# Opening a three-part kernel another way, and placing a block's last output product inside the next block

## The chip, the cores and the metric

The kernel runs on 1 core of one Trainium2 chip. The metric is the device time of one execution in microseconds. Before the change three runs took 1523.68 to 1529.89 us, with a median of 1525.85 us. All arithmetic is in fp32; a matrix product is either done on whole fp32 operands (such a matmul stands as one in the program and as two in the trace) or as three products of operands cut into a high and a low part.

## The reference, cut to what matters

Three parts follow one another. The first is a two-way attention between a sequence `x` (8 batches, 8 heads, 512 positions, 64 columns) and a small state (32 rows per head); its output has 8 x (512 + 32) rows of 512 columns. The second is a gated MLP with 1536 hidden columns, the third an MLP with 2048.

```python
scores = scale * np.matmul(x, state.transpose(0, 1, 3, 2))
scores = scores - scores.max(-1, keepdims=True)
a = np.exp(scores)
a /= a.sum(-1, keepdims=True) + 1e-09
xread = np.matmul(a, state)
scores2 = scale * np.matmul(state, x.transpose(0, 1, 3, 2))
...
sread = np.matmul(a2, x)
return np.concatenate([xread, sread], axis=2).astype(np.float32)

g = x @ w_gate
silu = g * (1.0 / (1.0 + np.exp(-g)))
val = x @ w_val
return (silu * val @ w_out).astype(np.float32)

h = x @ w_in
g = h * (1.0 / (1.0 + np.exp(-1.702 * h)))
return (g @ w_out).astype(np.float32)
```

The weights of the two MLPs arrive as 64-bit floats and are turned into fp32 on the chip.

## The kernel before, in words

The work is split into nine blocks of rows: one for each batch's 512 positions (blocks 0 to 6, then 7 at the end) and, before the last, a block "B" with the 256 state rows of all batches. A block goes through 12 steps `f` of the first MLP. A step makes a gate product and a value product (`product`, the value one after the gate one, each into a `gv` bank of PSUM), takes Silu of the gate on ScalarE, multiplies on VectorE into `h`, cuts `h` into a high part (ScalarE) and a low part (VectorE, in block 0 GpSimd), and then issues the output product `out1` of the step before: four output tiles `acc0` to `acc3`, three matmuls of 128x512 each. The output product of step 11 closes the block; `evac` then copies the four tiles out and SyncE stores them. After the nine blocks the second MLP runs over the same blocks, from about 798 us to the end; the change does not touch it.

Attention for batch b+1 is prepared during block b. It is written in pieces: two groups of four heads, each with a load of `x` (`xn`), transpositions (`turn0`, `turn1`), scores (`scores0`, `scores1`, or `scores_full` for the first two batches), maxima along the state (`max_n`) and along the sequence (`max_s`), exponentials (`exp_n`, `exp_s`), sums, and the reads of the state. Three hand-written tables set the order: `START` lists what happens before block 0 (groups A0 and A1 of batch 0), `BLOCK0` places the pieces of batch 1, and of A0 and A1's remaining work, at places (f, 0), (f, 1), (f, 2) of block 0, and `GROUP` does so for all later batches. Place 0 comes after Silu, place 1 after the multiplication, place 2 after the output product. Every engine executes its own instructions strictly in the order in which they are written.

Three more things share these places. A `slot` (`whole_slot`) starts the 64-to-32-bit turn of one raw weight tile (two ScalarE activations, L200 and L201), finishes the one before (VectorE L209 and L210, GpSimd L213) and issues the load of another; block 0 has three slots in each step (`beside`), and before it START has its own. `state_weights` multiplies the turned gate and value weights (`wf`) with the state (`st`), since batch 0 multiplies attention weights with these products; each needs two turned tiles. A `quad_job` does the same for batches 1 to 7, with two PSUM tiles at a time; the lists `JOBS` say at which third of a step it stands, and a job at place 0 follows the pieces of `GROUP` at that place.

PSUM's eight banks are four `acc`, two `gv` and two `at`. Transpositions, scores, state products and quad jobs ask for an `at` tile through `at()`; a list `extra` lets `at()` hand out the `acc` banks too, until `extra.clear()` at the end of START.

SyncE and ScalarE issue the DMAs, each in its own order. Lines that the prediction speaks of: L426 transposes `xn`, L380 the raw state, L534 the exponentials of the state scores (`e`), whose copy to SBUF is `ec` at L537; L334 is any whole product; L624 a quad job; L446 and L447 the scores of a later batch; L327 to L329 gate and value products; L923 to L925 the output product; L948 is Silu, L961 the multiplication, L776 and L777 the cut of `h`; L487 and L488 are `max_s`, L502 is `exp_s`.

Of the kernel before, what the change touches and what calls it, by code (L numbers as in the profile page):

```python
# [8 lines left out]
F32 = mybir.dt.float32  # L9
# [8 lines left out]


START = """  # L20
A0.load0 A0.load1 states weights1 A1.load0 A1.load1 weights6 G0.load
A0.turn0 A0.turn_h0 A0.turn1 A0.turn_h1 attn_state slot slot A0.scores_full
A1.turn0 A1.turn_h0 A1.turn1 A1.turn_h1 slot A0.max_n A0.less_max:v A0.exp_n A1.scores_full slot
A1.max_n A1.less_max:v A1.exp_n slot sw0 A0.sum_n A0.over_sum:v A0.back_full sw1
A1.sum_n A1.over_sum:v A1.back_full slot slot A0.max_s A1.max_s A0.exp_s A1.exp_s slot
""".split()

BLOCK0 = {  # L30
    (0, 1): "A0.turn_e",
    (0, 2): "A1.turn_e",
    (1, 0): "G0.turn0 G0.turn_h0",
    (1, 1): "A0.state_read",
    (1, 2): "attn_state",
    (2, 0): "A0.state_sum A1.state_read G0.turn1 G0.turn_h1",
    (2, 2): "A1.state_sum G0.scores_full",
    (3, 0): "G0.max_n G0.max_s",
    (3, 2): "A0.state_store A1.state_store G0.less_max:v G0.exp_n G0.exp_s",
    (4, 0): "G0.sum_n G0.over_sum:v G0.turn_e",  # L40
# [14 lines left out]
}  # L55
GROUP = {
    (0, 1): "turn0 turn_h0 turn_l0:v",
    (1, 0): "scores0",
    (1, 1): "turn1 turn_h1 turn_l1:v",
    (1, 2): "scores1",  # L60
    (2, 0): "max_n",
    (2, 1): "less_max:v max_s",
# [10 lines left out]
def kernel(  # L73
# [29 lines left out]
    P = 128  # L103
    KD = DM // P
    F1 = FF1 // P
    U1 = F1 // 2
    F2 = FF2 // P
    J = S // P
# [5 lines left out]
    v, a, pe, pool_e, sy = nc.vector, nc.scalar, nc.tensor, nc.gpsimd, nc.sync  # L114
# [6 lines left out]
    dp = ctx.enter_context(tc.tile_pool(name="scratch", bufs=1, space=DRAM))  # L121
# [219 lines left out]
    def accs():  # L341
        return [psa.tile([P, 512], F32, name=f"acc{i}", tag=f"acc{i}") for i in range(4)]
# [25 lines left out]
    def load_states(qd, q=sy):  # L368
        sb["raw"] = sb_raw = ap.tile([P, HP, P], F32, name="sb_raw", tag="e2")
        for j in range(4):  # L370
            q.dma_start(
                sb_raw[j * NS : (j + 1) * NS].rearrange("n hp (hl d) -> n hp hl d", hl=2),
                state[4 * qd + j].rearrange("(hp hl) n d -> n hp hl d", hl=2),
            )
# [276 lines left out]
    def cut_fetched(b, u, g, home=None):  # L651
# [6 lines left out]

    JOBS = [
        [10, 14, 17, 20, 22, 24, 26, 29, 30, 31, 32, 33, 34, 35],  # L660
        [2, 6, 7, 8, 9, 10, 12, 13, 15, 17],
        range(0, 36, 3),
        range(0, 36, 3),
    ]
# [118 lines left out]
    def evac(acc, N):  # L783

        for e in range(0, len(acc), 2):
            ev = work.tile([P, 2, 512], F32, name="ev", tag="raw", bufs=RAWS)
            a.copy(ev[:, 0, :N], acc[e][:, :N])
            v.tensor_copy(ev[:, 1, :N], acc[e + 1][:, :N])
            yield e, ev

    def h_tile(n):
# [10 lines left out]
    groups[0, 0], groups[0, 1] = A0, A1  # L802
    groups[1, 0] = Group(1, 0, whole=True)
    named = {"A0": A0, "A1": A1, "G0": groups[1, 0]}
    more = {
        "attn_state": lambda: (turn_states(0), attn_state(0)),
        "slot": whole_slot,
        "sw0": lambda: state_weights(0, 0),
        "sw1": lambda: state_weights(0, 1),
        "states": lambda: load_states(0, a),  # L810
    }
    for n in range(1, 7):
        more[f"weights{n}"] = lambda n=n: w_dma(n)
    for word in START:
        piece(word, named, more)()
    extra.clear()

    tails = []

# [44 lines left out]
    def cut_units(u, ks=range(KD)):  # L864

        for k in ks:
# [2 lines left out]
            a.copy(w[:, 0, :], t)  # L869
            pool_e.tensor_tensor(w[:, 1, :], t, f32(w[:, 0, :]), op=ALU.subtract)  # L870

    order2 = [B] + list(range(B))
    for i, blk in enumerate(order1):
        tail = blk == B
# [20 lines left out]
        def run(f, place):  # L895
            move()
            for fn in plan.pop((f, place), []):
                fn()

        nxt = None  # L900
        if not last and order1[i + 1] == B:
            nxt = tail_x
        acc = [] if i == 0 else accs()
        hs = {}

        def out1(f, between=None, k0=0):
            if not acc:
                acc.extend(accs())
            if i == 0:
                need_whole(("o", 0, f))  # L910
                cut_outs()
            h = hs.pop(f)
            w = units["o", 0 if i == 0 and f == 1 else 1, f]
            pos["outs"] = f + 1
            for e in range(KD):
                c = slice(e * P, (e + 1) * P)
                ps = acc[e][:, :N]
                if i == 0 and f == 1:
                    pe.matmul(ps, w[:, c], f32(h[:, 0, :N]), start=f == 0, stop=f == F1 - 1)
                    if between and e % 2 == 1:  # L920
                        between(k0 + e // 2)
                    continue
                pe.matmul(ps, w[:, 0, c], h[:, 0, :N], start=f == 0, stop=False)  # L923
                pe.matmul(ps, w[:, 1, c], h[:, 0, :N], start=False, stop=False)  # L924
                pe.matmul(ps, w[:, 0, c], h[:, 1, :N], start=False, stop=f == F1 - 1)  # L925
                if between and e % 2 == 1:
                    between(k0 + e // 2)
# [14 lines left out]
        for f in range(F1):  # L942
# [3 lines left out]
            beside()  # L946
            sg = work.tile([P, 512], F32, name="sg", tag="sg")
            a.activation(sg[:, :N], pg[:, :N], ACTF.Silu)  # L948
            run(f, 0)
            if i == 0 and f % 2 == 1 and f < F1 - 2:  # L950
                state_weights(f // 2 + 1, 1)
# [30 lines left out]
                need(units2[min(NEW + 2 * f + 1, len(units2) - 1)][0])  # L982
                x2_step(0, f, 1)
        assert not plan
        out1(F1 - 1, nxt, 2)
        y1[blk] = []
        for e, ev in evac(acc, N):
            y = dp.tile([P, 2, N], F32, name=f"y1_{blk}_{e}")
            sy.dma_start(y, ev[:, :, :N])
            y1[blk].append(y)  # L990
        if i == 3:
            pos["limit"] = where["i2", 0]
            w_dma(2)
# [299 lines left out]
```

## Time and profile before

| | |
|---|---|
| median of 3 runs | 1525.85 us |
| profiled execution, its own time | 1525.99 us |
| span of its instructions | 1524.2 us |
| PE busy | 1484.9 us |
| DVE busy | 925.9 us |
| ACT busy | 686.1 us |
| POOL busy | 395.3 us |
| mean granted TensorE clock | 0.996 |

PE is TensorE's matmuls, PEld its weight loads, DVE VectorE, ACT ScalarE, POOL GpSimd, SP SyncE. The span runs from the first to the last instruction; the execution's own time is 1.8 us longer. A row of the timeline gives the start, the time it took, the engine, the line, the operation, what it writes and reads, and in brackets how long the engine sat idle before it and what ended that. Where rows of one kind follow each other they are merged and carry a count. PEclk is the granted clock, 1.00 for 2.4 GHz and 0.50 for 1.2 GHz; the records of it begin at 17.2 us, and a stretch before that reads 1.00 without a record.

### The profile page before, as it was taken

What the parts mean: (1) busy time and instruction counts of PE and PEld (TensorE: products, weight loads), DVE (VectorE), ACT (ScalarE), POOL (GpSimd) and SP (SyncE); (2) the same over time, 40 slices, a digit from 0 to 9 for tenths busy, and PEclk for the clock granted to TensorE, in tenths of its full rate; (3) what the DMA queues carried; (4) which work ended last, traced back from release to release, by engine and by line L of the source; (5) the groups of instructions that cost most, each with busy time, mean ns of one, the idle gap of its engine ahead of it and who ended that gap; (6) DMA issues with size and microseconds to landing.
All of it is one profiled execution on the core that took longest, in us unless ns stands there. A gap on an engine that the chain in (4) does not pass through costs nothing.

```text
span 1524.2 us, 21139 instructions
## 1 busy us (share of the span) xinstructions
PE 1484.9 (97%) x7692; PEld 1196.4 (78%) x7692; DVE 925.9 (61%) x1604; ACT 686.1 (45%) x1251; POOL 395.3 (26%) x325
## 2 busy tenths in 40 slices
PE   5999999999999999999999999999999999999998
PEld 2554567676678777789778888999999999999997
DVE  6876566566659797963334334656556565665554
ACT  5665544445447576754454432333323333233332
POOL 3565222222215453555665521000000000000000
PEclk9999999999999999999999999999999999999999
DMA  7563442334346565630766666466564656564553
GB/s 225 162 209 103 143 128 87 122 116 147 117 165 179 186 178 189 175 109 16 235 230 243 245 207 207 160 210 211 166 239 170 227 180 229 185 225 163 208 183 134
DMA packets 137040, 267.20 MB, mean 175 GB/s; under 512 B 46312, under 2 KB 57576, under 8 KB 136936
## 3 DMA queue, kind: packets, MB, share of 16 engines
q1 hardware_dynamic: 113240, 221.54, 44.4%
q10 hardware_dynamic: 23696, 44.31, 8.8%
q8 instruction: 61, 1.00, 0.3%
q14 instruction: 43, 0.35, 0.1%
HBM read 202.11 MB, written 63.70 MB: 174 GB/s over the span
## 4 chain that ended last, share of the span: by engine, by line
PE 50%; DVE 5%; DMA 4%; issue 3%; ACT 2%; POOL 2%; ACTq 0%; SPq 0%; POOLq 0%; DVEq 0%
PE acc L337 8%; PE acc L338 8%; PE acc L339 8%; PE gv L1194 4%; PE gv L1193 4%; PE gv L1192 3%; DMA xf<-sw 3%; PE at L1192 3%; PE at L1193 3%; PE at L1194 3%; PE gv L320 1%; PE gv L322 1%; PE gv L321 1%; POOL wu L870 1%; DVE sg L961 1%
## 5 line engine op out<-in xcount | busy, mean ns | idle before, releaser
L777 DVE TENSOR_TENSOR h<-sg,h 128x512 fp32r<-128x512 f32 (+1 forms) x240 | 196.1, 817 | 133.7 <-ACT h L776 131.5
L776 ACT CAST h<-sg 128x512 fp32r<-128x512 f32 (+1 forms) x251 | 149.8, 597 | 196.9 <-DVE sg L961 93.5
L337 PE MATMUL acc<-wo,h 128*128 128x512 f32 x512 | 200.6, 392 | 0.0
L338 PE MATMUL acc<-wo,h 128*128 128x512 f32 x512 | 200.6, 392 | 0.0
L339 PE MATMUL acc<-wo,h 128*128 128x512 f32 x512 | 199.2, 389 | 0.0
L656 POOL TENSOR_TENSOR xo<-xf,xo 128x512 fp32r<-128x512 f32 x84 | 112.1, 1338 | 250.9 <-ACT xo L655 217.9
L1216 ACT ACTIVATE sg<-wt 128x512 f32<-128x512 f32 x56 | 35.4, 632 | 300.1 <-DVE wt L1214 288.1
L923 PE MATMUL acc<-h,wu 128*128 128x512 f32 (+1 forms) x428 | 167.8, 392 | 2.7 <-ACT h L776 2.7
L925 PE MATMUL acc<-h,wu 128*128 128x512 f32 (+1 forms) x428 | 163.1, 381 | 1.6 <-DVE h L777 1.5
L924 PE MATMUL acc<-h,wu 128*128 128x512 f32 (+1 forms) x428 | 162.5, 380 | 0.0
L327 PE MATMUL gv<-a,xo 128*128 128x512 f32 x336 | 139.6, 415 | 3.7 <-ACT sg L948 3.1
L328 PE MATMUL gv<-a,xo 128*128 128x512 f32 x336 | 133.6, 398 | 0.0
L329 PE MATMUL gv<-a,xo 128*128 128x512 f32 x336 | 133.2, 397 | 0.0
L961 DVE TENSOR_TENSOR sg<-gv,sg 128x512 f32<-128x512 f32 (+1 forms) x107 | 70.4, 658 | 80.2 <-PE gv L329 26.4
L339 PEld LDWEIGHTS acc<-wo,h 128*128 128x128 f32 x512 | 96.2, 188 | 20.8
L337 PEld LDWEIGHTS acc<-wo,h 128*128 128x128 f32 x512 | 96.6, 189 | 17.1
L338 PEld LDWEIGHTS acc<-wo,h 128*128 128x128 f32 x512 | 96.6, 189 | 15.8
L1214 DVE TENSOR_TENSOR wt<-wt,gv 128x256 f32<-128x256 f32 x56 | 23.6, 421 | 136.4 <-PE gv L1194 136.4
L923 PEld LDWEIGHTS acc<-h,wu 128*128 128x128 f32 x428 | 80.7, 189 | 25.6 <-issue 7.5
L327 PEld LDWEIGHTS gv<-a,xo 128*128 128x128 f32 x336 | 63.3, 188 | 44.8 <-issue 22.9
L925 PEld LDWEIGHTS acc<-h,wu 128*128 128x128 f32 x428 | 80.5, 188 | 20.0 <-DVE h L777 4.2
L1194 PE MATMUL gv<-xo,wu 128*128 128x256 f32 x336 | 95.4, 284 | 0.0
(176 smaller groups left out, 3463.3 us busy)
## 6 DMA issues: line engine op xcount, KB each, us to landing
wo<-w2b SPq DMA_DIRECT2D x128, 512.0 KB
wc<-w2c SPq DMA_DIRECT2D x84, 512.0 KB
xf<-sw ACTq DMA_DIRECT2D x84, 256.0 KB
raw<-in_moe_w_out_dram SPq DMA_DIRECT2D x28, 512.0 KB
sw<-qs ACTq DMA_DIRECT2D x24, 512.0 KB
sw<-qs ACTq DMA_DIRECT2D x24, 384.0 KB
y<-ev SPq DMA_DIRECT2D x16, 512.0 KB
raw<-in_moe_w_in_dram SPq DMA_DIRECT2D x16, 512.0 KB
```

The lines of the kernel that those rows point to most:

```text
L327: pe.matmul(ps, wh, xh, start=k == 0, stop=False)
L328: pe.matmul(ps, wl, xh, start=False, stop=False)
L329: pe.matmul(ps, wh, xl, start=False, stop=k == len(pairs) - 1)
L337: pe.matmul(ps, lh, rh, start=first, stop=False)
L338: pe.matmul(ps, lh, rl, start=False, stop=False)
L339: pe.matmul(ps, ll, rh, start=False, stop=last)
L776: a.copy(h_, src)
L777: eng.tensor_tensor(l_, src, f32(h_), op=ALU.subtract)
L923: pe.matmul(ps, w[:, 0, c], h[:, 0, :N], start=f == 0, stop=False)
L924: pe.matmul(ps, w[:, 1, c], h[:, 0, :N], start=False, stop=False)
L925: pe.matmul(ps, w[:, 0, c], h[:, 1, :N], start=False, stop=f == F1 - 1)
L1194: pe.matmul(ps, w[:, 0, c], x_[:, 1, kt], start=False, stop=kt == 1)
```

## The change

There are four edits.

1. START loads each of the two groups of batch 0 with one DMA in place of four, both before any weight, and the state between them from ScalarE's queue. A new piece `warm` writes 32 transpositions of the identity matrix into one PSUM tile, ahead of the first transposition of data. `max_s` of A0 and A1 moves ahead of the two slots that it followed, and the last slot of START is left out.
2. `extra.clear()` moves from the end of START into the first `out1`, so `at()` hands out the four `acc` banks during step 0 and the beginning of step 1 of block 0. The table BLOCK0 places A0's and A1's remaining pieces up to one place earlier or more.
3. In GROUP `scores0` moves from place (1, 0) to (1, 1); in block 1 two quad jobs move from (0, 2) to (1, 0) and from (5, 2) to (6, 0).
4. The closing of a block (the output product of step 11, `evac` and the stores) becomes a function `close`. After blocks 0 to 5 and B it is called in the next block, right after the first Silu has been issued. After block 6, which is followed by B, and after the last one it is called at once, as before.

```diff
 START = """
-A0.load0 A0.load1 states weights1 A1.load0 A1.load1 weights6 G0.load
+A0.load states A1.load weights6 G0.load warm
...
-A1.sum_n A1.over_sum:v A1.back_full slot slot A0.max_s A1.max_s A0.exp_s A1.exp_s slot
+A1.sum_n A1.over_sum:v A1.back_full A0.max_s A1.max_s slot slot A0.exp_s A1.exp_s
 """.split()
 BLOCK0 = {
-    (0, 1): "A0.turn_e",
-    (0, 2): "A1.turn_e",
...
+    (0, 0): "A0.turn_e",
+    (0, 1): "A1.turn_e",
+    (0, 2): "A0.state_read",
...
 GROUP = {
-    (1, 0): "scores0",
-    (1, 1): "turn1 turn_h1 turn_l1:v",
+    (1, 1): "scores0 turn1 turn_h1 turn_l1:v",
...
-        [2, 6, 7, 8, 9, 10, 12, 13, 15, 17],
+        [3, 6, 7, 8, 9, 10, 12, 13, 15, 18],
...
+    def warm():
+        ps = at()
+        for n in range(32):
+            pe.transpose(ps[:, n % J * P : n % J * P + P], ident, ident)
...
-    extra.clear()
...
+    pending = []
...
-        acc = [] if i == 0 else accs()
+        acc = []
...
-        def out1(f, between=None, k0=0):
+        def out1(f, between=None, k0=0, i=i, N=N, acc=acc, hs=hs):
             if not acc:
+                extra.clear()
                 acc.extend(accs())
...
             a.activation(sg[:, :N], pg[:, :N], ACTF.Silu)
+            while pending:
+                pending.pop()()
             run(f, 0)
...
-        out1(F1 - 1, nxt, 2)
-        y1[blk] = []
-        for e, ev in evac(acc, N):
-            ...
+        def close(blk=blk, N=N, acc=acc, out1=out1, nxt=nxt):
+            out1(F1 - 1, nxt, 2)
+            y1[blk] = []
+            for e, ev in evac(acc, N):
+                ...
+        if last or nxt:
+            close()
+        else:
+            pending.append(close)
```

The order of TensorE's instructions from the start of the program to the first steps of block 0 was this (`xn` is loaded `x`, `sb_raw` the raw state, `st` the state as an operand, `wf` turned weights, `gv` the gate and value products, `e` the exponentials, `ec` their transposed copy):

```order
L426 MATMUL at<-ident,xn 128x128 x8
L380 MATMUL at<-ident,sb_raw 128x128 x4
...
L334 MATMUL at<-wf,st_97 128x512 x4
L334 MATMUL gv<-a,xo 128x512 x4
L534 MATMUL at<-ident,e_318 128x128 x4
L334 MATMUL at<-wf,st_97 128x512 x2
L534 MATMUL at<-ident,e_320 128x128 x4
L334 MATMUL gv<-a,xo 128x512 x2
L426 MATMUL at<-ident,xn 128x128 x4
L334 MATMUL at<-wf,st_97 128x512 x2
L334 MATMUL gv<-a,xo 128x512 x2
L334 MATMUL at<-xn,ec 128x256 x4
```

With the change it is this (line numbers shift by a few, so L333 is the old L334, L533 the old L534 and L930 the old L923):

```order
L808 MATMUL at<-ident 128x128 x32
L425 MATMUL at<-ident,xn 128x128 x8
...
L333 MATMUL at<-wf,st_97 128x512 x4
L333 MATMUL gv<-a,xo 128x512 x2
L533 MATMUL at<-ident,e_345 128x128 x4
L333 MATMUL gv<-a,xo 128x512 x2
L533 MATMUL at<-ident,e_347 128x128 x4
L333 MATMUL at<-wf,st_97 128x512 x2
L333 MATMUL at<-xn,ec 128x256 x4
L333 MATMUL gv<-a,xo 128x512 x2
L333 MATMUL at<-xn,ec 128x256 x4
L333 MATMUL at<-wf,st_97 128x512 x2
```

The transpositions of both `e` now stand around the second `gv` product of step 0, the two reads of the state (`xn,ec`) come in step 0 and step 1, and the state product of step 1 comes after them.

In step 1 of block 2 TensorE's order was this, from the gate product's last matmul through the scores and the quad job (`qt`) to the value product and the transposition:

```order
L329 MATMUL gv<-a,xo 128x512
L446 MATMUL at<-xth_2015,stc 128x512
L447 MATMUL at<-xtl_2017,stc 128x512
L624 MATMUL at<-wf,qt 128x512 x2
L327 MATMUL gv<-a,xo 128x512
...
L329 MATMUL gv<-a,xo 128x512
L426 MATMUL at<-ident,xn 128x128 x4
```

With the change it is:

```order
L328 MATMUL gv<-a,xo 128x512
L623 MATMUL at<-wf,qt 128x512 x2
L326 MATMUL gv<-a,xo 128x512
...
L328 MATMUL gv<-a,xo 128x512
L445 MATMUL at<-xth_2038,stc 128x512
L446 MATMUL at<-xtl_2040,stc 128x512
L425 MATMUL at<-ident,xn 128x128 x4
```

The quad job follows the gate product directly, and the two score matmuls stand six matmuls later, ahead of the second transposition.

At the end of block 4 TensorE's order was this, from the end of step 10's output product through step 11's to the first product of block 5:

```order
L925 MATMUL acc_3464<-h,wu 128x512
L923 MATMUL acc_3461<-h,wu 128x512
L924 MATMUL acc_3461<-h,wu 128x512
L925 MATMUL acc_3461<-h,wu 128x512
...
L925 MATMUL acc_3464<-h,wu 128x512
L327 MATMUL gv<-a,xo 128x512
L328 MATMUL gv<-a,xo 128x512
L329 MATMUL gv<-a,xo 128x512
```

With the change it is:

```order
L932 MATMUL acc_3572<-h,wu 128x512
L326 MATMUL gv<-a,xo 128x512
L327 MATMUL gv<-a,xo 128x512
L328 MATMUL gv<-a,xo 128x512
L326 MATMUL gv<-a,xo 128x512
L327 MATMUL gv<-a,xo 128x512
L328 MATMUL gv<-a,xo 128x512
L930 MATMUL acc_3569<-h,wu 128x512
L931 MATMUL acc_3569<-h,wu 128x512
```

The six matmuls of block 5's first gate product stand between the two output products of block 4.

## Rows read from the trace of the kernel before

**Rows 1.** The page's head: span, then busy time, share and instructions of TensorE

```profile
span 1524.2 us, 21139 instructions
PE 1484.9 (97%) x7692; PEld 1196.4 (78%) x7692; DVE 925.9 (61%) x1604; ACT 686.1 (45%) x1251; POOL 395.3 (26%) x325
```

**Rows 2.** Windows: stretch, length, busy us of PE, PEld, DVE, ACT, POOL; clock, DMA

```profile
0.00:44.50 44.50, 25.64 (x59) 12.11 (x60) 31.47 (x47) 26.97 (x48) 16.44 (x18) 0.92 0.74 218
44.50:163.60 119.10, 116.88 (x383) 61.48 (x382) 83.00 (x128) 70.44 (x124) 65.08 (x49) 1.00 0.51 155
```

**Rows 3.** Waits of PE, whole span: who for whom, us, times, longest

```profile
PE at L624 <- ACT qs L630: 2.7, 4, 0.7
PE acc L923 <- ACT h L776: 2.7, 2, 1.3
...
PE at L624 <- DVE xtl L439: 0.3, 1, 0.3
```

**Rows 4.** Timeline of PE, 0 to 46 us

```profile
5.30 1.94 PE L426 MATMUL at<-ident,xn 128*128 128x128 f32 x8 [5.30 <-DMA xn<-in_x_dram]
8.85 1.09 PE L380 MATMUL at<-ident,sb_raw 128*128 128x128 f32 x4 [1.61 <-DMA raw<-in_moe_w_val_dram]
11.35 3.78 PE L334 MATMUL at<-xth,st 128*128 128x512 f32 x4 [1.42 <-ACT st L389]
...
24.34 2.07 PE L334 MATMUL at<-wf,st 128*128 128x512 f32 x2 [2.50 <-POOL wf L213]
...
28.76 2.81 PE L334 MATMUL gv<-a,xo 128*128 128x512 f32 x6 [0.82 <-ACT wt L200]
33.42 0.66 PE L534 MATMUL at<-ident,e 128*128 128x128 f32 x4 [1.85 <-ACT e L502]
33.92 1.88 PE L334 MATMUL at<-wf,st 128*128 128x512 f32 x4
41.07 1.10 PE L534 MATMUL at<-ident,e 128*128 128x128 f32 x4 [5.27 <-ACT ec L537]
41.96 3.17 PE L334 MATMUL gv<-a,xo 128*128 128x512 f32 x4
```

**Rows 5.** Windows, as Rows 2, for the stretch after TensorE's wait at 24 us

```profile
24.10:27.40 3.30, 3.06 (x4) 1.00 (x4) 3.09 (x8) 0.95 (x2) 0.18 (x1) 0.50 0.54 158
```

**Rows 6.** Tile xn, 0 to 140 us: ns of one issue, least, median, most

```profile
L420 SPq DMA_DIRECT2D xn<-in_x_dram x8: 547/630/708, 0.7 to 7.1; - x8
```

**Rows 7.** Timeline of DVE, 11 to 49 us

```profile
13.61 1.66 DVE L210 SCALAR_TENSOR_TENSOR wf<-raw,wf 128x512 uint32<-128x512 uint32 x1
...
28.54 0.39 DVE L209 TENSOR_SCALAR wf<-wf 128x512 uint32<-128x512 uint32 x1
28.96 0.69 DVE L210 SCALAR_TENSOR_TENSOR wf<-raw,wf 128x512 uint32<-128x512 uint32 x1
...
31.60 0.67 DVE L487 TENSOR_REDUCE sm<-ST 128x1 f32<-128x512 f32 x1
...
33.16 0.42 DVE L209 TENSOR_SCALAR wt<-wt 128x512 uint32<-128x512 uint32 x1
```

**Rows 8.** Timeline of ACT, 0 to 70 us

```profile
32.55 0.72 ACT L502 ACTIVATE e<-ST,sm 128x512 f32<-128x512 f32 x1 [3.29 <-DVE sm L488]
...
38.83 0.60 ACT L948 ACTIVATE sg<-gv 128x512 f32<-128x512 f32 x1
```

**Rows 9.** Timeline of POOL, 11 to 64 us

```profile
13.31 1.41 POOL L213 TENSOR_TENSOR wf<-wf,raw 128x512 uint32<-128x512 uint32 x1 [12.01 <-DVE wf L210]
...
31.81 1.28 POOL L213 TENSOR_TENSOR wf<-wf,raw 128x512 uint32<-128x512 uint32 x1 [0.68 <-DVE wf L210]
...
39.99 1.29 POOL L213 TENSOR_TENSOR wf<-wf,raw 128x512 uint32<-128x512 uint32 x1 [0.69 <-ACT wt L200]
```

**Rows 10.** Timeline, step 1 of block 2

```profile
261.61 1.12 PE L624 MATMUL at<-wf,qt 64*128 64x512 f32 x2 [0.68 <-ACT qs L630]
```

**Rows 11.** Timeline, end of block 4

```profile
516.72 0.50 PE L923 MATMUL acc<-h,wu 128*128 128x512 f32 x1 [1.35 <-ACT h L776]
```

More of the change, by code (lines that the diff above doesn't have):

```diff
@@ L24 @@
 A1.max_n A1.less_max:v A1.exp_n slot sw0 A0.sum_n A0.over_sum:v A0.back_full sw1
-A1.sum_n A1.over_sum:v A1.back_full slot slot A0.max_s A1.max_s A0.exp_s A1.exp_s slot
+A1.sum_n A1.over_sum:v A1.back_full A0.max_s A1.max_s slot slot A0.exp_s A1.exp_s
 """.split()
 BLOCK0 = {
-    (0, 1): "A0.turn_e",
-    (0, 2): "A1.turn_e",
[L33 to L37, printed above, removed]
+    (0, 0): "A0.turn_e",
+    (0, 1): "A1.turn_e",
+    (0, 2): "A0.state_read",
+    (1, 0): "A0.state_sum A1.state_read",
+    (1, 1): "G0.turn0 G0.turn_h0",
+    (1, 2): "A1.state_sum attn_state G0.turn1 G0.turn_h1",
+    (2, 2): "G0.scores_full",
     (3, 0): "G0.max_n G0.max_s",
@@ L810 @@
         "states": lambda: load_states(0, a),
+        "warm": warm,
     }
@@ L984 @@
         assert not plan
-        out1(F1 - 1, nxt, 2)
-        y1[blk] = []
-        for e, ev in evac(acc, N):
-            y = dp.tile([P, 2, N], F32, name=f"y1_{blk}_{e}")
-            sy.dma_start(y, ev[:, :, :N])
-            y1[blk].append(y)
+        def close(blk=blk, N=N, acc=acc, out1=out1, nxt=nxt):
+            out1(F1 - 1, nxt, 2)
+            y1[blk] = []
+            for e, ev in evac(acc, N):
+                y = dp.tile([P, 2, N], F32, name=f"y1_{blk}_{e}")
+                sy.dma_start(y, ev[:, :, :N])
+                y1[blk].append(y)
+        if last or nxt:
+            close()
+        else:
+            pending.append(close)
         if i == 3:
```

## The prediction

> **What bounds the kernel now.** First the page's head and the table by stage [rows 1, 2]: the reader is to see a TensorE that is busy for 1484.9 of 1524.2 us. All that an edit of the order can win is the other 39.3 us, and work that runs at half clock. By stage that idle time is 44.50 - 25.64 = 18.9 us up to 44.5 us, 119.10 - 116.88 = 2.2 in the rest of block 0, and the other 18.2 lie in the 1360 us behind it. Second the waits [rows 3]: outside the opening they are many short ones with names, above all four of 0.7 us ahead of a quad job and two of 1.3 us ahead of an output product. Third the opening's timeline [rows 4], in which each wait ends on another engine: DMA (5.30), the state's landing (1.61), ScalarE's state copies (1.42), turned weights (2.50), exponentials (1.85), a copy out of PSUM (5.27). Fourth the clock. Four 128-column transpositions took 0.66 us at 33.42 but 1.09 at 8.85 and 1.10 at 41.07; four passes of a whole product took 1.88 at 33.92 and 3.78 at 11.35 [rows 4]. So TensorE works at half clock in three stretches: before its first long run, after the wait at 24 us (granted 0.50 [rows 5]) and after the one of 5.27.
>
> **Opening: loads and warm transpositions.** Eight issues of 0.63 us on SyncE become two for A0 and A1, with the weights behind [rows 6]: SyncE gains 6 x 0.63 = 3.8 us. That moves no end by itself. A0 now lands as one piece, later than its first half did; but TensorE's next need is the raw state, at 8.85, and its landing hangs on ScalarE's queue, which keeps its four issues. The warm piece is 32 transpositions, at half clock (1.94 - 1.09) / 4 = 0.21 us each since eight took 1.94 and four 1.09 [rows 4]: 6.8 us, from the identity's completion at about 1.4 us to 8.2. A0's eight then take 1 us to 2 us and end at 9.2 to 10.3, against 7.2 before; since the state could not start before 8.85, the price is 0.4 to 1.4 us if nothing else changed, and this is the worst end. The gain is that the scores at 11.35 no longer take 3.78 but 1.88. What is late next is VectorE: its merge at 13.61 is stretched to 1.66 and ends at 15.27 [rows 7], so the first maxima cannot begin 1.9 us earlier, only some 0.8, and the same chain (maxima of A0, merge, maxima of A1, merge, sums) then runs on one engine up to 28.54 without a gap over 0.5 us. I take 1.1 us for the end of that chain, between -1.4 and 1.9.
>
> **Opening: maxima first, free banks, one slot less.** The maxima run from 31.60 to 33.16 behind two merges that start at 28.54 [rows 7]. Moved ahead, they start at 28.54 - 1.1 = 27.4 and A0's exponential, 0.9 us behind its reduction's start [rows 7, 8], at 28.4 in place of 32.55, so TensorE's transposition follows at 29.3 instead of 33.42. It stands between the two products of step 0, which end at 31.6 as before (28.76 + 2.81 [rows 4]). Price: the two merges slide by 1.56 - 1.1 = 0.5 us, and the second turned tile is ready at 33.6 instead of 31.81 + 1.28 = 33.1 [rows 9]; the state product of step 1 waits for it, so it ends at about 34.7 against 35.8. The second transposition no longer waits 5.27 us for `ec`, since `at()` now has another bank for it, and it goes ahead of that state product. Silu stood behind two turned tiles and a wait for GpSimd; 6.3 us passed from A0's exponential to it [rows 8], with two tiles turned and a cut that waited for GpSimd; one tile and the cut (some 2.1 us) now stand behind it, so it comes at 28.4 + 4.2 = 32.6, not 38.83. Then TensorE has, without waiting: the first state read (34.7 to 36.5), the gate product of step 1 (to 38.2), the second state read (to 40.1). What is late next is GpSimd: it has the same cuts and merges to do, with no lead. The tile that ended at 39.99 + 1.29 = 41.3 [rows 9] ends at about 42.0 now, because the cut of `h` goes ahead of it; the state product waits 1.1 us for it and ends at 43.0. Value product, transposition, output product and second transposition follow up to 48.4. In the trace TensorE is through the same work at 57.35, with one product more (1.7) that now comes later: 55.6. The lead is 7.2 us. It holds the 5.27 and 1.85 waits and the half clock after the former (1.10 + 3.17 against 0.66 + 1.88 [rows 4], 1.7 us).
>
> VectorE and GpSimd reach that point with a lead of 0 to 3 us only. Up to the end of block 0 they have 119.10 - 83.00 = 36 and 54 us without work [rows 2], so they can catch up, with some waits. I take 6.5 us for the opening. Its low end is 1.1 us, if the pace of VectorE's chain is passed on to all of block 0; its high end is 10, near half of the 18.9 us of idle time.
>
> The trace shows the clock falling after TensorE's wait of 2.50 us [rows 4, 5], and in my schedule that wait is still 2.4 us long. The Trainium skill, "TensorE: Matmul & The Clock Gate", Part 1 (The HAM clock gate), says that the throttled state is the default and that idleness brings it back, which speaks against warming up ahead of waits. By it the two products at 25 and 27.6 us would run at half clock again; the first of them waits for VectorE anyway, so the sum would lose 1 us at most.
>
> The second half of a merge took 0.69 us at 28.96 but 1.66 at 13.61, and there GpSimd's own from 13.31 on lay beside it [rows 7, 9]. The skill's "SBUF — State Buffer", Who interferes with whom, says that a VectorE operation with two SBUF inputs blocks while GpSimd reads SBUF, or the reverse. The rows agree: 1.0 us more beside GpSimd. A denser opening would by that rule stretch more merges; four of them would bring the opening down from 6.5 to 2.5.
>
> **Quad jobs.** The job at place 0 asked for the bank of the scores just ahead of it, whose copies come late on VectorE: 0.68 us idle, four times in blocks 2 and 3 [rows 3, 10], and 0.3 in block 1. With the scores behind the value product, the job meets banks that were emptied a gate product (1.6 us) earlier. All five waits go: 3.0 us. The scores' own consumers are an output product (2.9 us) away. Bounds: 0 to 3.0.
>
> **Closing a block later.** TensorE's instructions are the same. At the ends of blocks 4 and 5 it waited for ScalarE's part of `h`, 1.35 and 1.34 us [rows 3, 11]; now the next block's gate product, six matmuls or 1.4 us, runs there. That gate product needs only a bank that Silu has left, and operands cut in step 10. At the ends of blocks 0 to 3 and B there is no wait, so nothing to win. Price: the four copies of `evac` stand behind the next Silu and ahead of that block's first multiplication, on ScalarE and VectorE, and the stores move with them on SyncE. Behind them wait the multiplication and, through `h`, the output product one step later. Their cover is the value product that follows (1.4 us) and the whole of step 1; if that cover failed, 0.7 us would be late at each of seven boundaries, 4.9 us. I take the gain of 2.7, between -4.9 + 2.7 = -2.2 and 2.7.
>
> **Sum.** 6.5 + 3.0 + 2.7 = 12.2 us. The span goes from 1524.2 to 1512.0, the profiled execution from 1525.99 to 1513.8; that execution stands 0.1 us above the median of the runs, so I forecast 1513.7 us.
>
> **Rivals.**
> (a) The opening's lead is taken back: VectorE and GpSimd set the pace of block 0, and only their 1.1 us arrive. For it: GpSimd's turned tile at 42.0 is later than before, and VectorE had no gap in the opening. Against: 36 us of free VectorE in the rest of block 0. 1525.85 - 1.1 - 3.0 - 2.7 = 1519.1.
> (b) The warm piece does not bring the full clock to the first scores, because TensorE waits again behind it. Then A0 is 1.4 us late and the scores cost 3.78 again: the chain loses 2.5 us, and the total gain is 9.7: 1516.2. The same time comes out if `evac` spoils the boundaries (9.5).
> (c) The slot missing from START makes every turned tile one slot later in block 0, and the state products of steps 1, 3, 5, 7 and 9 wait for it. A late tile costs at least a merge and GpSimd's part, 0.42 + 1.66 + 1.28 = 3.4 us [rows 7, 9]; five are 17 us, less 12.2: 1530.5, slower. It decides from 2.4 us a step. Against: in the trace these products had their tiles early enough that the whole rest of block 0 shows 2.2 us idle.
> (d) The opening gives its upper end: 1525.85 - 10 - 5.7 = 1510.2, and a little more if the clock never falls.
>
> **Chances.** Forecast 0.54 (its own range 1510.5 to 1517), (a) 0.17, (b) 0.13, (c) 0.06, (d) 0.10. The range from 1507.5 to 1520 takes in (a), (b) and (d). A measurement of this kernel can tell about 0.5%, 7.6 us, from no change: the line is 1518.2. The forecast, (b) and (d) lie below it, and a fifth of (a): faster 0.79, within it 0.16, slower 0.05.
>
> **What would show it.** Right: no wait over 1 us of the second `e` transposition, Silu of step 0 before 34 us, TensorE through the first output product and the second `xn` transposition behind it at 46 to 50 us; no wait at a quad job in blocks 2 and 3; gate products of blocks 5 and 6 directly behind step 10's output product, and output products behind them without a gap. Wrong: waits on GpSimd's turned tiles in steps 1 to 9, a granted clock of 0.50 from 10 to 17 us, waits of the first output product of a block for an `acc` bank or for `h`.

## The result, and the profile after

The changed kernel takes 1513.27 us (median of 4 runs, 1512.51 to 1514.82); the kernel before took 1527.28 us on the same chip (4 runs, 1523.68 to 1529.89). The ratio is 0.9911, with a 95% interval from 0.9887 to 0.9935. The forecast of 1513.7 us fits. The experiments show that its terms do not: the opening gave far less than was forecast, the quad jobs far more. The profiled execution took 1512.51 us; its span is 1524.2 - 1510.7 = 13.5 us shorter than before, where 12.2 were forecast.

The page's head of the changed kernel, against [rows 1]:

```profile
span 1510.7 us, 21191 instructions
PE 1481.1 (98%) x7724; PEld 1198.7 (79%) x7724; DVE 924.7 (61%) x1604; ACT 686.3 (45%) x1251; POOL 395.0 (26%) x325
```

Here are three windows of the changed kernel, with the columns of [rows 2]. The first two meet at the same place in the work as 47.1 us before; the third is inside the second.

```profile
0.00:43.30 43.30, 32.98 (x112) 19.26 (x113) 32.05 (x48) 27.57 (x49) 16.05 (x18) 0.92 0.74 213
43.30:163.60 120.30, 115.49 (x370) 60.25 (x369) 83.25 (x128) 70.93 (x125) 65.81 (x49) 0.99 0.53 159
50.30:53.50 3.20, 3.12 (x9) 2.47 (x10) 1.08 (x2) 0.00 (x0) 1.29 (x1) 0.50 0.61 199
```

TensorE's idle time in the opening fell from 18.9 to 43.30 - 32.98 = 10.3 us. Most of that fall is no gain: 5.9 us of it are the warm transpositions, which begin while TensorE before still waited for its first load, and whose results nothing reads. Behind the opening, idle time rose from 2.2 to 4.8 us, with a stretch at half clock. TensorE's waits name the new one, to be held against [rows 3]:

```profile
PE gv L326 <- ACT sg L955: 3.4, 4, 1.4
PE acc L930 <- DVE srd L568: 3.3, 1, 3.3
PE at L333 <- POOL wf L212: 3.0, 2, 2.2
PE acc L932 <- DVE h L776: 2.8, 4, 0.9
...
PE acc L930 <- ACT h L775: 0.3, 1, 0.3
```

The four waits ahead of quad jobs are gone. Of the 2.7 us that output products waited for ScalarE's part of `h`, 0.3 us are left. New is one wait of 3.3 us for `srd`. TensorE's timeline shows the opening and that wait (lines of the changed kernel: L333 is any whole product, L533 the `e` transposition, L930 to L932 the output product):

```profile
1.36 5.86 PE L808 MATMUL at<-ident 128*128 128x128 f32 x32 [1.36 <-POOL ident masks.py:199]
...
9.95 1.98 PE L333 MATMUL at<-xth,st 128*128 128x512 f32 x4 [1.42 <-ACT st L388]
...
29.32 0.79 PE L533 MATMUL at<-ident,e 128*128 128x128 f32 x4 [0.47 <-ACT e L501]
29.91 3.48 PE L333 MATMUL gv<-a,xo 128*128 128x512 f32 x4
33.22 0.60 PE L533 MATMUL at<-ident,e 128*128 128x128 f32 x4
...
42.38 1.12 PE L333 MATMUL at<-wf,st 128*128 128x512 f32 x2 [0.81 <-POOL wf L212]
43.34 1.88 PE L333 MATMUL gv<-a,xo 128*128 128x512 f32 x4
...
50.38 0.76 PE L930 MATMUL acc<-h,wu 128*128 128x512 f32 x1 [3.32 <-DVE srd L568]
50.94 0.63 PE L931 MATMUL acc<-h,wu 128*128 128x512 f32 x1
```

The 32 warm transpositions took 5.86 us (forecast 6.8). Up to 43.34 us the schedule worked out by hand holds within 0.8 us but for one place: 29.3 us forecast for the first `e` transposition, no wait at the second, a wait of 1.1 forecast against 0.81. The exception is the end of step 0's two products, 33.2 us where 31.6 was forecast; the granted clock was 0.50 from 29.7 to 33.1 us, and the row at 29.91 took 3.48 us. ScalarE's and VectorE's rows agree (forecast: maxima 27.4, exponential 28.4, Silu 32.6):

```profile
27.53 0.64 DVE L486 TENSOR_REDUCE sm<-ST 128x1 f32<-128x512 f32 x1
```

```profile
28.45 0.72 ACT L501 ACTIVATE e<-ST,sm 128x512 f32<-128x512 f32 x1 [1.13 <-DVE sm L487]
...
32.49 0.60 ACT L955 ACTIVATE sg<-gv 128x512 f32<-128x512 f32 x1
```

Then the first output product stops at its third tile, `acc2`. That bank had been lent by `at()` to `A1.state_read`, and its reader, `A1.state_sum` (L568), stands in VectorE's order behind the multiplication and a merge:

```profile
46.23 0.68 DVE L968 TENSOR_TENSOR h<-gv,sg 128x512 f32<-128x512 f32 x1
46.84 1.21 DVE L208 TENSOR_SCALAR wf<-wf 128x512 uint32<-128x512 uint32 x1
48.08 0.69 DVE L209 SCALAR_TENSOR_TENSOR wf<-raw,wf 128x512 uint32<-128x512 uint32 x1
...
49.06 1.16 DVE L568 TENSOR_SCALAR srd<-at,sm 32x64 f32<-32x64 f32 x4
```

It ends at 50.22, the output product goes on at 50.38, and the six matmuls that are left run at the granted clock of 0.50 of the third window (0.63 us in place of 0.39).

How far TensorE is ahead can be followed through the program. Both kernels make the same 3120 gate and value matmuls in the same order. The start of the n-th in the kernel before, less its start in another kernel, is that kernel's lead. All columns but the first lead belong to experiments below, and each is of one profiled execution:

| time before, us | changed | e4 | e9 | e10 | e11 | e12 |
|---|---|---|---|---|---|---|
| 41.96 | 4.86 | 4.67 | 0.14 | 5.43 | 5.51 | 4.74 |
| 53.31 | -0.45 | 4.33 | 0.43 | -0.29 | 0.14 | 4.40 |
| 84.91 | 1.71 | 5.92 | 0.44 | 1.54 | 1.56 | 6.01 |
| 228.39 | 2.27 | 6.60 | 0.36 | 1.38 | 2.11 | 6.64 |
| 277.18 | 5.54 | 9.88 | 3.67 | 2.91 | 5.41 | 9.91 |
| 433.19 | 10.77 | 15.10 | 8.87 | 2.80 | 10.66 | 15.10 |
| 646.30 | 14.59 | 18.65 | 13.44 | 2.40 | 12.09 | 19.02 |
| 737.42 | 13.55 | 17.32 | 12.84 | 1.78 | 10.27 | 17.19 |
| 798.98 | 13.15 | 13.15 | 11.65 | 2.42 | 14.29 | 21.21 |
| 1494.02 | 13.48 | 12.96 | 12.04 | 2.10 | 14.13 | 21.09 |

In the changed kernel the opening leaves 1.71 us. Blocks 1 to 3, where the quad jobs stand, bring the lead to 10.77, and the rest of the program 2.7 more.

A quad job shows why. Its two matmuls have 64 rows each, and the trace counts two records for each. These rows are of the kernel before: a job without a wait, the first half of the job whose second half is in [rows 10], and what follows it:

```profile
254.81 1.13 PE L624 MATMUL at<-wf,qt 64*128 64x512 f32 x4
255.87 0.50 PE L327 MATMUL gv<-a,xo 128*128 128x512 f32 x1
...
259.81 1.12 PE L624 MATMUL at<-wf,qt 64*128 64x512 f32 x2
...
262.66 0.53 PE L327 MATMUL gv<-a,xo 128*128 128x512 f32 x1
```

And the job of the changed kernel that takes the place of the second:

```profile
257.07 1.20 PE L623 MATMUL at<-wf,qt 64*128 64x512 f32 x4
258.19 0.51 PE L326 MATMUL gv<-a,xo 128*128 128x512 f32 x1
```

In the job without a wait all four records fit in 255.87 - 254.81 = 1.06 us: the halves run side by side. Where the second half waited, the first took 1.12 us alone, TensorE idled 0.68, and the second took its 1.12 alone: 262.66 - 259.81 = 2.85 us from start to start, against 258.19 - 257.07 = 1.12 in the changed kernel. The idle time was less than half of what the wait cost. The last three of the four jobs gave 1.74 or 1.75 us of lead each. The first gave 3.30, since in the kernel before a stretch at half clock followed it (263.0 to 266.4 us).

Two things lie beside these four. The job of block 1 whose wait was 0.28 us in the kernel before (at 168.83 us) took 2.41 us from start to start there, and the one in its place takes 1.10. And not every such loss shows as a wait: ten of the changed kernel's 48 jobs still take 1.37 to 2.27 us (the one at 188.05 us takes 2.27) with no wait of TensorE named in the profile, where the others take 1.03 to 1.13. That is some 6 us; why they do was not tested.

### The profile page after: what moved, and what is told of

Its sections match the earlier page's. It is cut to its first block, busy times and chain, and to the rows that moved or that the text cites. A ratio compares the mean times of both kernels' runs of the same rounds, so it can differ in the third digit from the quotient of the medians.

```text
span 1510.7 us, 21191 instructions
## 1 busy us (share of the span) xinstructions
PE 1481.1 (98%) x7724; PEld 1198.7 (79%) x7724; DVE 924.7 (61%) x1604; ACT 686.3 (45%) x1251; POOL 395.0 (26%) x325
## 4 chain that ended last, share of the span: by engine, by line
PE 57%; DMA 5%; DVE 4%; ACT 2%; issue 1%; ACTq 0%; POOL 0%; DVEq 0%; POOLq 0%; SPq 0%
PE acc L336 8%; PE acc L337 8%; PE acc L338 8%; DMA xf<-sw 4%; PE gv L1210 4%; PE gv L1209 4%; PE gv L1208 4%; PE at L1208 3%; PE at L1209 3%; PE at L1210 3%; PE gv L326 2%; PE gv L327 1%; PE gv L328 1%; PE gv L320 1%; PE gv L321 1%; PE gv L319 1%
## 5 line engine op out<-in xcount | busy, mean ns | idle before, releaser
L655 POOL TENSOR_TENSOR xo<-xf,xo 128x512 fp32r<-128x512 f32 x84 | 111.6, 1332 | 238.3 <-ACT xo L654 226.8
L930 PE MATMUL acc<-h,wu 128*128 128x512 f32 (+1 forms) x428 | 167.8, 392 | 3.6 <-DVE srd L568 3.3
L932 PE MATMUL acc<-h,wu 128*128 128x512 f32 (+1 forms) x428 | 163.6, 382 | 3.0 <-DVE h L776 2.8
L1230 DVE TENSOR_TENSOR wt<-wt,gv 128x256 f32<-128x256 f32 x56 | 23.6, 421 | 136.8 <-PE gv L1210 136.8
L930 PEld LDWEIGHTS acc<-h,wu 128*128 128x128 f32 x428 | 80.8, 189 | 26.3 <-issue 10.4
L932 PEld LDWEIGHTS acc<-h,wu 128*128 128x128 f32 x428 | 80.8, 189 | 21.5 <-DVE h L776 5.6
```

## The experiments

They ran in three sets (e1 to e4, e5 to e8, e9 to e12), the second on another chip. The median of the kernel before was 1525.46, 1524.85 and 1527.05 us in them, so medians across sets agree only to some 2 us; ratios and intervals are against the kernel before of the same set, and the gains in us beside them follow from the ratios. The changed kernel's own 1513.27 us are from a set ahead of these three.

**e1, the quad jobs alone.** In the kernel before:

```diff
-    (1, 0): "scores0",
-    (1, 1): "turn1 turn_h1 turn_l1:v",
+    (1, 1): "scores0 turn1 turn_h1 turn_l1:v",
...
-        [2, 6, 7, 8, 9, 10, 12, 13, 15, 17],
+        [3, 6, 7, 8, 9, 10, 12, 13, 15, 18],
```

> The kernel before with the third edit alone (scores0 moved to place (1, 1), two quad jobs of block 1 moved). Theory: a quad job whose second half waits 0.68 us for its bank also loses the overlap of its two halves (about 1.06 us), so each of the four jobs in blocks 2 and 3 gives back about 1.74 us, block 1 some 0.5, and the drop of the clock behind the first of them goes too: 7 to 9 us faster than before. Rival (the prediction's term): only the idle time goes, 3.0 us.

1517.00 us, ratio 0.9948 (0.9935 to 0.9960): 8 us faster, 6.1 to 9.9. The theory holds, the prediction's 3.0 falls. Its trace ends with a lead of 11.17 us.

**e2, the closing alone.** The function `close` and its call behind Silu, in the kernel before.

> The kernel before with the fourth edit alone (the closing of a block deferred into the next block's first step). Theory: the two waits of 1.35 us at the ends of blocks 4 and 5 go, and part of it is given back at new waits in the blocks behind: 0.7 to 2.7 us faster. Rival: the copies of the closing spoil the next block's first steps, no gain or up to 2.2 us slower.

1524.86 us, ratio 0.9991 (0.9978 to 1.0004): 1.4 us faster, between 3.4 faster and 0.6 slower. It doesn't tell the theory from no gain. Its trace ends with a lead of 1.95 us.

**e3, the opening alone.** START, `warm`, the later `extra.clear()` and BLOCK0, in the kernel before.

> The kernel before with the first two edits alone (START, the warm piece, the later extra.clear, BLOCK0). Theory: the lead of about 5 us that TensorE has at 42 us is mostly lost when the first output product waits 3.3 us for a lent bank and then runs at half clock, so only about 1.7 us are left: 1 to 2.5 us faster. Rival (the prediction's term): 6.5 us faster.

1526.69 us, ratio 1.0005 (0.9995 to 1.0015): nothing, 0.8 us faster at most. The prediction's 6.5 falls, and the theory's 1 to 2.5 was too much. Its trace has the same wait of 3.33 us at the first output product, and a longer stretch at half clock behind it (49.7 to 56.5 us). It ends with a lead of 0.46 us.

**e4, the lent bank read out early.** In the changed kernel:

```diff
-    (1, 0): "A0.state_sum A1.state_read",
+    (1, 0): "A0.state_sum A1.state_read A1.state_sum",
...
-    (1, 2): "A1.state_sum attn_state G0.turn1 G0.turn_h1",
+    (1, 2): "attn_state G0.turn1 G0.turn_h1",
```

> The changed kernel with A1.state_sum moved from place (1, 2) to (1, 0), so that the bank acc2 which A1.state_read was lent is read out before the first output product wants it. Theory (the lent bank is what takes the opening's lead): the wait of 3.32 us and the half clock behind it go, and 2 to 5 us of the lead are kept, 1508 to 1511 us. Rival (VectorE and GpSimd set the pace of block 0): the wait turns up at another place in steps 1 to 4 and the time stays within 0.7 us of the changed kernel.

The wait is gone, as TensorE's timeline of e4 shows; `state_sum` ends ahead of the multiplication on VectorE:

```profile
47.18 0.39 PE L930 MATMUL acc<-h,wu 128*128 128x512 f32 x1
...
48.55 0.60 PE L425 MATMUL at<-ident,xn 128*128 128x128 f32 x4
```

```profile
45.18 1.17 DVE L568 TENSOR_SCALAR srd<-at,sm 32x64 f32<-32x64 f32 x4
...
48.17 0.68 DVE L968 TENSOR_TENSOR h<-gv,sg 128x512 f32<-128x512 f32 x1
```

The lead at 84.91 us is 5.92 us in place of 1.71, and 4.1 us of the difference are still there at 646 us. But the time is 1512.13 us, ratio 0.9918 (0.9904 to 0.9932), the same as the changed kernel's. So VectorE's pace is not what took the opening's lead, and half of the theory falls too: the lead doesn't reach the end. It goes in block 7, between 737 and 799 us. There ScalarE's casts of loaded state weights (`xo<-xf`, L654) wait for the load, and Silu and TensorE behind them:

```profile
767.67 0.62 ACT L654 CAST xo<-xf 128x512 fp32r<-128x512 f32 x1 [4.50 <-DMA xf<-sw]
768.19 0.61 ACT L223 CAST wu<-raw 128x512 fp32r<-128x512 f32 x1
768.71 0.59 ACT L955 ACTIVATE sg<-gv 128x512 f32<-128x512 f32 x1
```

```profile
769.35 0.50 PE L326 MATMUL gv<-a,xo 128*128 128x512 f32 x1 [2.61 <-ACT sg L955]
```

In the changed kernel that cast came at 769.22, only 1.55 us later, though its TensorE was 3.8 us further back at 737 us. So when TensorE goes on, at 769.35 us in e4 and at 770.91 in the changed kernel, 1.56 of the 3.8 us are left. From 769.9 to 773.3 us e4 runs at half clock, which the changed kernel does not, and at the end of that stretch the lead over it is 0.03 us. The waits for loads took 2.2 us of the lead, the clock the rest.

**e5, no warm piece.** In e4:

```diff
-A0.load states A1.load weights6 G0.load warm
+A0.load states A1.load weights6 G0.load
```

> e4_sum_early without the warm piece. Theory: the first scores run at half clock again (3.8 us in place of 2.0), the chain of maxima behind them comes 0.8 to 1.5 us later, and the lead that e4 shows at 80 us shrinks by 1 to 2 us; of that 0.5 to 2 reach the end, 1512.6 to 1514.1 us. Rival: the warm piece delays the first transpositions by as much as it gains and the clock falls at 16 us in any case, so the lead at 80 us stays within 0.5 us, 1511.6 to 1512.6 us.

1513.54 us, ratio 0.9922 (0.9908 to 0.9936), and no difference of lead over 0.11 us at any place from 79 to 480 us: the rival's reading, nothing gained. The median lies in the theory's range, but the intervals of e4 and e5 are nearly the same. The scores do run at half clock; the first row is e5, the second e4:

```profile
11.28 3.75 PE L333 MATMUL at<-xth,st 128*128 128x512 f32 x4 [1.42 <-ACT st L388]
```

```profile
10.02 1.98 PE L333 MATMUL at<-xth,st 128*128 128x512 f32 x4 [1.42 <-ACT st L388]
```

But the first instruction of the maxima stands behind two merges on VectorE, and starts at 15.69 us in e5 and 15.61 in e4:

```profile
14.93 0.69 DVE L209 SCALAR_TENSOR_TENSOR wf<-raw,wf 128x512 uint32<-128x512 uint32 x1
15.69 0.71 DVE L481 STREAM_TRANSPOSE sp<-ST 128x512 f32<-128x512 f32 x1
```

```profile
15.00 0.69 DVE L209 SCALAR_TENSOR_TENSOR wf<-raw,wf 128x512 uint32<-128x512 uint32 x1
15.61 0.70 DVE L481 STREAM_TRANSPOSE sp<-ST 128x512 f32<-128x512 f32 x1
```

**e6, the loads of blocks 2 to 7 earlier.** In e4:

```diff
-                    put(2 * u - 3, g + 1, fetch, b, u, g)
+                    put(2 * u - 3, 0 if b > 1 else g + 1, fetch, b, u, g)
```

> e4_sum_early with the loads of state weights (xf) of blocks 2 to 7 issued at place 0 of their step in place of places 1 and 2, 2 to 4 us earlier. Theory: e4's lead of 4.3 us at 680 us is given back where ScalarE's casts wait for xf (up to 4.5 us each in block 7) and Silu stands behind them; with earlier loads 1.5 to 4 us of it reach the end, 1508 to 1510.6 us. Rival: the landings are set by the DMA queues' bandwidth, or the issues wait for buffers and hold ScalarE up: no gain, 1511.5 to 1513.5 us.

1511.28 us (1509.62 to 1513.72), ratio 0.9910 (0.9897 to 0.9924): within what can be told of e4 and of the changed kernel. Behind the first pairs of block 7 the issues hardly move. Each pair of loads has two buffers, and its two issues are held back in different ways. The first stands behind a cast in ScalarE's own order: here it comes at 743.02, right behind the start of the cast at 742.92 that had waited 3.82 us for a load, though its buffer's last reader (GpSimd, L655) had ended at 738.20 + 1.29 = 739.5. The second comes at 745.00, when that cast's buffer has been read by GpSimd as well. These are e6's rows; e4's cast came at 742.38:

```profile
738.20 1.29 POOL L655 TENSOR_TENSOR xo<-xf,xo 128x512 fp32r<-128x512 f32 x1 [1.73 <-ACT xo L654]
```

```profile
742.92 0.62 ACT L654 CAST xo<-xf 128x512 fp32r<-128x512 f32 x1 [3.82 <-DMA xf<-sw]
743.02 0.52 ACTq L648 DMA_DIRECT2D xf<-sw  x1
...
745.00 0.51 ACTq L648 DMA_DIRECT2D xf<-sw  x1
```

**e7, the changed kernel without the deferred closing.** `close` is called at once in every block.

> The changed kernel with every block closed at its own end, as before. Theory: the closing is worth the same beside the other edits as alone, 1 to 2.7 us: 1514.3 to 1516 us. Rival: in the changed kernel what it gains at the ends of blocks 4 and 5 is taken back where ScalarE waits for xf: 1512.8 to 1513.8 us.

1517.07 us, ratio 0.9945 (0.9932 to 0.9957), a median 3.8 us above the changed kernel's. In the traces the deferred closing is worth 0.5 us of lead at 433 us and 3.7 at 737. So the theory's sign holds, and its size was low. That the closing gives more beside the other edits than alone isn't shown: e2's interval reaches 3.4 us.

**e8, both halves of a quad job on the same rows.** In the changed kernel:

```diff
-            r = slice(hl * 64, hl * 64 + 64)
+            r = slice(0, 64)
```

> The changed kernel in which the second matmul of each of the 48 quad jobs reads rows 0 to 63 of its operands too, where it read rows 64 to 127 (that half of the products is then a copy of the other). The number of matmuls is the same. Theory: the two matmuls of a job run side by side because they use different halves of TensorE's rows, and on the same half they follow each other: 48 x 1.06 = 51 us slower than the changed kernel, 1564 us. Rival: a job's halves share the time anyway, and only the wait of 0.68 us counted in the kernel before: 1513.3 us, at most 2 more.

1547.99 us, ratio 1.0151 (1.0135 to 1.0168): 34.7 us above the changed kernel. The rival falls. The size was forecast 51 us; serial halves follow each other more closely than I had it, and ten of the changed kernel's jobs were not wholly side by side to begin with. The row of one job is

```profile
266.99 1.98 PE L623 MATMUL at<-wf,qt 64*128 64x512 f32 x4
268.90 0.50 PE L326 MATMUL gv<-a,xo 128*128 128x512 f32 x1
```

that is 1.91 us in place of 1.06, and 48 x 0.85 = 41 us at most. Behind the last job e8's trace is 455.27 - 424.05 = 31.2 us later than the changed kernel's. The span of its profiled execution is 1549.4 - 1510.7 = 38.7 us longer; part of what comes later is a stretch at half clock from 805.7 to 812.5 us.

**e9, edits 3 and 4 without the opening.**

> The kernel before with edits 3 and 4 (scores0 and the two quad jobs, the closing), and none of the opening. Theory (what the opening gains is lost at waits for DMA hundreds of us later, above all in blocks 5 and 7): the whole difference is there without it, 1512.5 to 1515 us. Rival (the prediction's term of 6.5 us, or the 4.3 us that the same groups would have without the lent bank): 1517 to 1520 us.

1514.12 us, ratio 0.9923 (0.9908 to 0.9938): the theory's range. Beside edits 3 and 4 the opening is worth 0.9 us by the medians, which is within their noise, and 13.48 - 12.04 = 1.4 in the traces.

**e10, the changed kernel without edit 3.**

> The changed kernel with edit 3 taken back (scores0 at (1, 0), the two quad jobs at their old places). Theory: the four jobs are worth 1.74 us each and the clock that falls behind the first of them 1.5 us, beside the other edits as alone: 7 to 9 us slower than the changed kernel, 1520.3 to 1522.3 us. Rival (the prediction's 3.0 us): 1516.3 us.

1524.81 us, ratio 0.9985 (0.9976 to 0.9994): 11.5 us slower by the medians, more than the theory's 7 to 9. In the traces the four jobs make 7.1 us of it again (1.75, 1.82, 1.75, 1.76). The waits of 0.68 us are back, but the clock stays at 1.00 behind the first of them, where it fell to 0.50 in the kernel before. (e2 and e3 have the same waits: it fell in e2, from 262.8 to 266.2 us, and not in e3.) The rows are e10's, and its window behind that job:

```profile
258.46 1.12 PE L624 MATMUL at<-wf,qt 64*128 64x512 f32 x2
260.26 1.12 PE L624 MATMUL at<-wf,qt 64*128 64x512 f32 x2 [0.68 <-ACT qs L630]
```

```profile
262.00:266.00 4.00, 4.00 (x21) 3.28 (x20) 2.11 (x4) 1.20 (x2) 0.00 (x0) 1.00 0.27 78
```

Much of the rest comes in blocks 4 to 6 (8.0 us of difference at 433, 12.2 at 646), above all at two waits that the changed kernel has shorter or not: 1.37 us for VectorE's part of `h` (574.71) and 1.42 for `e` (615.67).

**e11, the changed kernel with few loads in block 7.** `fetch` is left out there for the pairs behind the second, and the casts read the second pair's tile.

> The changed kernel, in which block 7 loads the state weights (xf) of its first two pairs of steps only; the later pairs use those of the second, so eight loads of 256 KB are left out and that block's results are others. Theory: TensorE's waits for Silu in block 7 (1.28, 0.33, 0.44 and 1.38 us in the changed kernel) come from ScalarE's casts that wait for these loads; without the loads 2.5 to 3.5 us go, 1509.8 to 1510.8 us. Rival: ScalarE waits for the raw weights of the second MLP on the same queues, and the waits stay: 1513 us.

1510.95 us, ratio 0.9889 (0.9875 to 0.9902), 2.3 us below the changed kernel's median; the two intervals overlap. Between 737 and 799 us the lead grows by 4.0 us, where the changed kernel's shrinks by 0.4. TensorE's waits of block 7 (700 to 790 us) are

```profile
PE acc L931 <- ACT h L776: 0.7, 1, 0.7
PE acc L933 <- DVE h L777: 0.7, 1, 0.7
```

with none for Silu. Here the theory was right in block 7; 2.5 us less lead at 646 us hide most of it, so that the trace ends only 0.65 us ahead of the changed kernel's.

**e12, e11 with the bank read out early.**

> e11_few_loads with A1.state_sum moved to (1, 0) as in e4_sum_early. Theory: e4's lead, which was 4.3 us at 680 us and is gone at 790, is lost at the loads of block 7, so beside e11 it reaches the end: 2.5 to 4 us faster than e11, 1506 to 1508 us. Rival: it is lost in the blocks ahead of block 7 or to chance landings, and e12 is within 1.2 us of e11.

1505.43 us (1502.97 to 1507.79), ratio 0.9855 (0.9841 to 0.9870): 5.5 us below e11, whose runs lie from 1508.44 to 1511.85. The lead of 4.45 us that e12 has over e11 at 84.91 us is 6.96 at the end; some 2.2 of that is a wait for `e` in block 5 (at 530.74) that e11 has and e12 hasn't. The same edit that was worth nothing in e4 arrives in full when block 7 doesn't wait for its loads.

Of the kernels with the whole computation e6 has the lowest median (1511.28 us), e4 is next; neither can be told from the changed kernel.

## Why the prediction was right, and where it was not

The time was right by luck, because two wrong sizes cancelled: 6.5 + 3.0 + 2.7 against, in the changed kernel's trace, 1.7 in block 0, 9.1 in blocks 1 to 3 and 2.7 behind them, 13.5 in all. The last of these is not a measure of the closing by itself: the lead reaches 14.59 us at 646 us, and block 7 takes part of it back.

**Opening, 6.5 us forecast, 1.7 measured at 85 us and about 1 at the end.** Nearly every row of the hand schedule came true, and e4 has 5.92 us at 85 us. The step that failed is that of the free banks: I used `at()`'s other banks for the second `e` transposition (rightly, the 5.27 us are gone) and put their return at nothing. "What would show it" named the sign (a first output product that waits for an `acc` bank); no term asked which of the lent tiles is read last. Rival (a) had the right size by a wrong mechanism: e4 shows that VectorE and GpSimd keep up. Rival (c) shows in one place, the wait of 0.81 us for a turned tile in step 1; the later steps have none. Second, I carried the lead to the end of the program as if nothing on the way ran at a pace of its own. e4, e11 and e12 show that block 7 does: what is won ahead of it is spent there, at waits for the landings of `xf` and, in e4, at half clock.

The warm piece gave nothing (e5): the 1.8 us saved on the scores ended in VectorE's queue. The chain of maxima did come 1.0 us earlier, where 1.1 was forecast (27.53 against 28.54 us), but e5 without the piece and e4 with it are alike (27.91 and 27.82); which part of START made it was not separated. Rival (b) is wrong in both halves: the piece did bring full clock to the scores, and without it nothing is lost. The rule of the Trainium skill weighed in the prediction ("TensorE: Matmul & The Clock Gate", Part 1) agrees with the trace: the clock fell to 0.50 at 16.05 us, behind the wait of 1.87 us at 12.8, and a warm-up ahead of waits bought nothing. It is not the same in every execution. In e8, e10 and e11, which have the same START, this wait took 0.86 to 1.61 us and the clock stayed at 1.00 up to 23.6 us or later. The two products that the prediction feared for (25 and 27.6 us) ran at 1.00 in the changed kernel, whose clock was back from 19.5 to 29.7 us.

The other fear, merges stretched beside GpSimd, came to little: up to 48 us five second halves of a merge take 1.66 us in the changed kernel, four in the kernel before. The last two of the five (38.08 and 41.22 us) lie shortly ahead of the state product of step 1 whose wait of 0.81 us is shown above.

**Quad jobs, 3.0 us forecast, 8 alone and 11.5 beside the other edits.** That the waits would go was right, and the size was off. The step that failed is "0.68 us idle, four times": it priced the wait by the idle time alone, as it did for the 0.3 us in block 1, a job that gave 1.3. [Rows 10] already held the other part: two records in 1.12 us, where a job without a wait has four in 1.06. The real price is 1.74: 0.68 of idle time and 1.06 of lost overlap, of which e8, with no wait, shows 0.85. In the profiled execution of before a fall of the clock from 263.0 to 266.4 us came on top. It is not there in e10 with the same waits, so I don't count it as their price.

The Trainium skill, "TensorEngine Tiling (Array Packing)", Key Properties, states that different tiles of the array can run matmuls in parallel. The rows agree, 1.06 against 1.91 us. That a wait of the second tile's matmul gives this up stands in the rows alone.

**Closing, 2.7 us forecast, 1.4 alone (-0.6 to 3.4) and 3.8 left out.** Right in mechanism, and in size as far as it can be told: the waits for ScalarE's `h` at the ends of blocks 4 and 5, 2.7 us, are gone, and the output product follows the next block's gate product without a wait:

```profile
504.38 0.40 PE L328 MATMUL gv<-a,xo 128*128 128x512 f32 x1
504.71 0.50 PE L930 MATMUL acc<-h,wu 128*128 128x512 f32 x1
```

The 0.3 us that are left stand at 718 us, in the first steps of block 7. The feared price, copies late at each boundary, does not show: TensorE's waits there are 0.28 + 0.65 us with the closing deferred and 0.33 + 0.54 us in e7.

**What stays open.** By the ratios the three parts alone make 7.9 + 1.4 - 0.8 = 8.5 us, together 13.6, and each of these figures is known to 1.5 to 4 us. By the leads at the end of the traces they make 11.17 + 1.95 + 0.46 = 13.6 alone and 13.5 together. So it isn't shown that the parts help each other. Blocks 4 to 7 hold short waits (for `e`, `h`, `sg`, 0.4 to 2.2 us) that come and go from one kernel to the next, and shift by 2 us even between kernels that are the same there (e11 and the changed kernel at 646 us). I did not separate what of that is a true interplay and what chance landings. Whether block 7 is held by ScalarE's order, in which an issue stands behind a cast that waits, by the two `xf` buffers or by the traffic beside them isn't settled either: e11 takes away all three, and neither an issue ahead of the cast nor a third buffer was tried.

The Trainium skill, "DMA: Bandwidth & Descriptors", Issuing engines are not separate DMA queues, says that loads issued from ScalarE and from SyncE share the same 16 engines. By it the traffic would count; no run here changes it alone.

## What to carry to other kernels

Price a wait from start to start of the whole job, against the same job without a wait; idle time misses what the wait un-overlaps. When a buffer is lent early, find the last reader of each loan in its engine's queue, and compare it with the time at which the owner wants it back. And before a lead won at the start is added to the total, look for a later stage that goes by its own landings: time won ahead of it can be spent waiting in it.

## What the runs showed of the hardware

- Two fp32 matmuls of 64 rows, on different halves of the rows and in different banks, took 1.06 us together, on the same half 1.91 us.
- The granted clock fell to 0.50 at 769.94 us in e4, 0.6 us behind a wait of TensorE of 2.61 us, and at 50.18 us in the changed kernel, in the last 0.2 us of a wait of 3.32. It did not fall behind e11's wait of 2.21 us (which ended at 530.74) or behind the changed kernel's waits of 1.09 to 1.38 us in blocks 5 to 7. After the wait of 0.68 us between two half-row matmuls it fell in the kernel before and in e2, and not in e3 and e10.
- e12, whose waits behind 24 us are all under 1.5 us, kept the clock at 1.00 from 32.6 us to its end. e11 kept it from 54.6 us to its end with one wait of 2.21.
